# The first head group's queries in two transfers and two sums, and a new order of the opening's steps

## The chip, the cores and the metric

One core of a Trainium2 chip runs the whole program. The metric is the device time of one execution in microseconds (us), median of the runs. TensorE (PE in the views; PEld is its weight load), VectorE (DVE), ScalarE (ACT) and GpSimd (POOL) each work through their own instruction list in order. SyncE (SP) issues nearly all transfers, also in order.

## What is computed

Two things follow one another: an attention with 32 landmarks over 4 batches, 8 heads, 576 positions and 64 features, and then two feed-forward layers over 2304 tokens.

```python
q_lm, k_lm = means of q and k over 18 neighbouring positions   # 32 landmarks
A, Bm, C = softmax(q k_lm^T), softmax(q_lm k_lm^T), softmax(q_lm k^T)
Z = Bm^T / (norm1(Bm) * normInf(Bm))
for _ in range(6):
    Z = 2 * Z - Z @ Bm @ Z
x = A @ Z @ C @ v
h = x @ w_in;   x = (h * tanh(softplus(h))) @ w_out            # first layer
h = x @ w_in2;  out = maximum(h, 0)**2 @ w_out2                # second layer
```

## The kernel before

The order of all work is written out by hand: `PROGRAM` is one string of 2641 steps, and the loop at the end of the function calls them one by one. An engine's instruction list is therefore the order in which the steps of the string issue to it. No scheduler moves anything afterwards. A step reads `thing.step@room+n`: `@` names the PSUM buffer (h and y have two each, at has one), and `+n` puts n filler products of the identity matrix with itself ahead of the step on TensorE; each of them shows as two records of L312.

The things are these. The letters a to h are head groups, two per batch, with four heads each. A group's steps are: `lq`, `lk`, `lv` (loads, L492 to L528), `sq`, `sk` (landmark sums on VectorE, L547 to L563), `hq`, `hk` (the same sums begun on GpSimd, L530), `Sq`, `Sk` (a copy of a sum on ScalarE), `tq`, `tk`, `tl` (transposes on TensorE, L590, L613, L614), `Tq`, `Tk`, `TL` (their results copied out by ScalarE), `pa`, `pb`, `pc` (scores for A, Bm and C on TensorE), `cm`, `ce`, `cr` (maximum, exp and reciprocal sum for C), `pe`, `ET`, `pv`, `cv` (C times v), and `at`, `am`, `mi`, `ae`, `su`, `mu`, `tb`, `ah`, `al` (softmax of A and its split into a high and a low part). `B0`, `B1`, `B2` are the inverses: batch 0, batch 1, and batches 2 and 3 together. Their steps are `bx`, `be`, `bs` (softmax of Bm), `nr` and `rs` (norms), `n0` to `n5` with `r` and `z` (the six iterations: a product on TensorE, a copy on ScalarE, a sum on VectorE), `pw` and `wz`. `F00` and its like fold Z, C and v into the first weight matrix (`fo` on TensorE, `mh` on ScalarE, `ml` on VectorE). `p0`, `p1` and so on are chunks of the first layer's first product (`f` on TensorE, tile hc; `M` on ScalarE), `t0`, `t1` and so on its second product (`y` on TensorE, `e` adding the result to acc on ScalarE or VectorE). `U0` to `U63` are weight units of 512 KB that arrive as packed words and are turned into floats by `lo` (ScalarE), `st` (VectorE), `ab`, `cl` and `ad`. The second layer's steps begin with W, X, Q, K, Y and Z.

The opening, up to the first chunk p0, is a mesh of short steps on all engines. The first group a needs its queries and keys, the transposes, the sums, the transposed sums, then the three score products. Group a's queries are one transfer of 128x1152 floats into one half of a ring buffer, and one reduction on VectorE sums them.

Of the kernel before, what the change touches and what calls it, by code (L numbers as in the profile page):

```python
# [19 lines left out]
P = 128  # L20
# [34 lines left out]
    c.xq b.cm d.lk a.cv B0.n0@at B0.r0 B0.z0 B0.n1@y+3 U3.d@m e.lq c.zq U3.lo b.lv b.mi b.ae U1.cl U1.ad B0.r1 b.ce
    U3.st U3.ab B0.z1 B0.n2@at b.su U3.cl U3.ad b.pe@h+2 b.cr b.mu B0.r2 B0.z2 c.TL c.pc@h+1 U4.hi U4.lw d.sk b.ET
    B0.n3@y c.pb@at c.PB b.tb B0.r3 B0.z3 b.pv@y b.cv e.sq d.Sk c.pa@at B0.n4@y b.ah c.at B0.r4 B0.z4 U7.ad U7.hi c.am
    a.al d.tk@h d.tl@y+3 U5.d U5.lo c.cm B0.n5@y d.Tk d.TL d.pb@y d.PB B1.bx B0.z5 d.pc@at d.cm b.al c.ce f.lk B1.be
    B1.bs e.lk f.tk@h f.Tk d.ce d.cr c.pe@h c.ET U6.d@gh B0.pw@y B0.wz U5.st e.tk@h e.Tk B1.nr@y U5.ab B1.rs U5.cl
    U0.ad F00.fo@h F00.mh d.pe@at d.ET B1.n0@y+2 B1.z0 d.pa@at B1.r0 F00.ml U6.lo U6.st U8.d U8.lo B1.n1@y B1.z1 U8.st  # L60
    U5.ad U5.hi p0.f0 p0.f1 B1.r1 p0.f2 p0.f3 d.at U6.ab U6.cl U6.ad U8.ab p0.M0 B1.n2@y U7.lw d.am B1.z2 B1.r2 d.lv
    U6.hi p0.M1 f.lq d.pv@y f.sq B1.n3@y f.tq@at B1.r3 B1.z3 f.Tq U6.lw p0.c0 e.sk p0.g0 e.tq@h B1.n4@y e.Tq p1.f0
    B1.r4 p1.f1 p1.f2 p1.f3 d.cv U5.lw B1.z4 B1.n5@at e.Sq c.lv p0.c1 p0.g1 e.Sk e.tl@y c.pv@y p1.M0 p1.c0 c.cr B1.z5
    U11.d p1.M1 e.TL p1.g0 U8.cl U8.ad p1.c1 p1.g1 e.pb@at e.PB c.cv e.pc@h e.cm U11.lo B1.pw@y c.mi B1.wz e.ce c.ae
    f.sk c.su t0.y0 t0.e0 t0.y1 f.Sk f.Sq f.tl@at d.mi d.ae d.su f.TL e.pe@h t0.e1 f.pb@y e.ET f.pa@at f.at c.mu
    f.pc@h c.tb U9.d F10.fo@h U11.st U9.lo U9.st f.PB F10.mh c.ah d.mu c.al e.lv d.tb d.ah f.cm F10.ml U11.ab d.al
    U11.cl U9.ab U9.cl e.pa@at t0.y2 f.ce e.at e.am f.cr t0.y3 p2.f0 p2.f1 p2.M0 p2.c0 p2.f2 p2.g0 U9.ad p2.f3 p2.M1
    p2.c1 p3.f0 p2.g1 t0.e2 p3.f1 p3.M0 g.lk g.sk g.lq U10.d g.tk@at t1.y0 g.Tk U11.ad t0.e3 U10.lo U10.st U10.ab
    U13.d g.tq@at U10.cl p3.c0 f.pe@h t1.y1 p3.f2 p3.f3 U13.lo g.Sk t1.e0 f.ET g.Tq U13.st U13.ab p3.g0 U10.ad
    F01.fo@h U13.cl F11.fo@at t1.e1 F01.mh t1.y2 F11.mh U12.d U12.lo F01.ml U13.ad U13.hi U12.st U12.ab t1.y3 p4.f0  # L70
    p3.M1 p3.c1 F11.ml g.sq p4.f1 p4.f2 g.Sq p4.M0 U13.lw e.cr p3.g1 t1.e2 t1.e3 p4.f3 g.tl@y U12.cl p4.c0 p4.g0 g.TL
    p4.M1 p4.c1 p5.f0 p5.f1 g.pa@at g.pb@y U12.ad f.am U12.hi g.at g.am g.PB p5.M0 U12.lw U14.d U14.lo U14.st U14.ab
    e.pv@y+1 g.mi e.cv g.pc@at g.cm U14.cl f.lv t2.y0 p4.g1 g.ce h.lk h.sk p5.f2 p5.f3 p5.M1 U14.ad t2.y1 t2.e0 f.mi
    U15.d U14.hi h.lq t2.e1 U15.lo U15.st U15.ab U15.cl h.sq t2.y2 t2.e2 h.tk@at h.Tk h.Sk g.lv t2.y3 t2.e3 U14.lw
    g.ae g.su h.tq@at p6.f0 U15.ad U15.hi p5.c0 p5.c1 p5.g0 p6.f1 p6.f2 p5.g1 p6.f3 h.Sq h.Tq h.tl@y h.TL f.pv@y f.cv
    U31.d@T h.pb@y h.PB U15.lw B2.bx B2.be h.pc@at h.cm p6.M1 t3.y0 t3.e0 B2.bs e.mi t3.y1 t3.y2 t3.e1 h.ce U21.d
    U21.lo U17.d U21.st U21.ab h.pa@h U17.lo U17.st t3.e2 B2.nr@y t3.y3 B2.rs f.ae e.ae e.su p6.M0 B2.n0@at e.mu p6.c0
    h.at B2.r0 B2.z0 p7.f0 p7.f1 p6.c1 p6.g0 p6.g1 p7.M0 B2.n1@y B2.r1 B2.z1 p7.f2 h.lv p7.f3 p7.c0 h.am h.mi B2.n2@y
    B2.r2 B2.z2 p7.M1 h.pe@h h.ET h.cr p7.c1 g.pe@at g.ET t3.e3 f.su B2.n3@y B2.z3 B2.r3 U21.cl U21.ad t4.y0 t4.e0
    t4.y1 B2.n4@at t4.e1 B2.z4 B2.r4 h.pv@y g.pv@y B2.n5@at g.cr U17.ab g.cv h.cv e.tb p7.g1 p7.g0 h.ae B2.z5 t4.y2  # L80
    x.m f.mu U31.lo B2.pw@at B2.wz t4.y3 f.tb f.ah U30.d@T f.al t4.e2 h.su e.ah e.al t4.e3 F20.fo@at F20.mh F20.ml
    h.mu F30.fo@h F30.mh F30.ml t5.y0 t5.y1 x.e p8.f0 p8.f1 p8.f2 p8.f3 F21.fo@at t5.e1 p8.M0 p8.c0 p8.g0 t5.e0 g.mu
    t5.y2 g.tb g.ah U21.hi U31.st h.tb g.al p8.M1 h.ah h.al U31.ab p8.c1 p8.g1 t5.e2 U21.lw p9.f0 p9.f1 p9.M0 p9.f2
# [1396 lines left out]
```

## Time and profile before

| | us |
|---|---|
| median of 3 runs | 773.5 (773.37 to 775.24) |
| the profiled execution: device time | 775.11 |
| its span, first to last instruction | 773.3 |
| TensorE busy | 758.2 (98%) |
| VectorE busy | 599.3 (78%) |
| ScalarE, GpSimd busy | 377.3, 384.7 |

The profiled execution is 1.6 us above the median, and 1.8 us of it lie outside the span. A record of a TensorE instruction reaches to its modelled end, and its successor starts before that. The distance from start to start is what one costs in a dense stretch. The granted TensorE clock is 0.999 over the whole span. In a row of the timeline the first number is the start and the second the duration, both in us, and square brackets give the engine's idle time just before and what ended it.

### The profile page before, as it was taken

The numbers are of one execution on the slowest core, as the hardware profiler recorded it, in microseconds if no ns is written. First come the engines' busy times: TensorE is split into PE (matmuls) and PEld (weight loads), VectorE is DVE, ScalarE is ACT, GpSimd is POOL, SyncE is SP. The second block draws the span as 40 slices with busy tenths as digits, with TensorE's granted clock in tenths as the row PEclk, the third lists the DMA queues.
The fourth block names the chain that finished last, engine by engine and source line by source line (L and its number), as shares of the span: only waits on it lengthen the run. The fifth ranks groups of instructions, "written<-read, shape, count | busy, mean of one in ns | idle before, by whom it ended". The sixth has DMA issues, their size and how long they took to land.

```text
span 773.3 us, 15445 instructions
## 1 busy us (share of the span) xinstructions
PE 758.2 (98%) x5926; PEld 709.2 (92%) x5926; DVE 599.3 (78%) x966; ACT 377.3 (49%) x624; POOL 384.7 (50%) x269
## 2 busy tenths in 40 slices
...
GB/s 324 205 196 161 83 178 141 3 42 114 87 87 82 150 151 224 212 232 223 213 139 282 260 283 272 272 309 257 256 312 333 240 246 271 215 241 253 279 197 83
DMA packets 87721, 156.73 MB, mean 203 GB/s; under 512 B 9184, under 2 KB 37088, under 8 KB 87648
## 3 DMA queue, kind: packets, MB, share of 16 engines
...
## 4 chain that ended last, share of the span: by engine, by line
PE 89%; DVE 4%; ACT 3%; DMA 2%; issue 1%; SPq 0%; DVEq 0%; ACTq 0%
PE y L951 8%; PE y L953 8%; PE y L952 8%; PE P L1304 7%; PE P L1305 7%; PE P L1306 7%; PE O L953 4%; PE O L952 4%; PE O L951 4%; PE hc L951 4%; PE hc L952 4%; PE hc L953 4%; PE O L1379 3%; PE O L1378 3%; PE O L1377 3%; PE m L933 2%
## 5 line engine op out<-in xcount | busy, mean ns | idle before, releaser
L1198 POOL TENSOR_TENSOR ringglx<-A,ringghx 128x768 fp32r<-128x768 f32 x40 | 78.7, 1985 | 61.9 <-ACT ringghx L1193 57.1
L1002 DVE TENSOR_TENSOR ringglx<-sc,ringghx 128x576 fp32r<-128x576 f32 (+2 forms) x80 | 58.1, 747 | 18.8 <-ACT ringghx L997 18.1
L953 PE MATMUL O<-b,ringglx 128*128 128x256 f32 x240 | 67.8, 282 | 0.0
L952 PE MATMUL O<-b,ringghx 128*128 128x256 f32 x240 | 67.8, 282 | 0.0
L951 PE MATMUL O<-b,ringghx 128*128 128x256 f32 x240 | 67.7, 282 | 0.0
L1193 ACT CAST ringghx<-A 128x768 fp32r<-128x768 f32 x40 | 32.8, 835 | 69.6 <-DVE A L1175 28.9
L1036 DVE TENSOR_TENSOR acc<-acc,y 128x384 f32<-128x384 f32 x72 | 38.9, 548 | 32.7 <-PE y L953 32.6
L984 ACT ACTIVATE sc<-hc 128x576 f32<-128x576 f32 x64 | 41.4, 650 | 43.5 <-PE hc L953 39.5
L1334 DVE TENSOR_TENSOR U<-U,P 128x384 f32<-128x384 f32 x72 | 39.6, 552 | 27.8 <-PE P L1306 26.5
L997 ACT CAST ringghx<-sc 128x576 fp32r<-128x576 f32 (+2 forms) x80 | 44.7, 578 | 13.3 <-PE y L953 12.3
L953 PEld LDWEIGHTS O<-b,ringglx 128*128 128x128 f32 x240 | 45.8, 191 | 0.0
L952 PEld LDWEIGHTS O<-b,ringghx 128*128 128x128 f32 x240 | 45.8, 191 | 0.0
L951 PEld LDWEIGHTS O<-b,ringghx 128*128 128x128 f32 x240 | 45.7, 190 | 0.0
L1334 DVE TENSOR_TENSOR A<-U,P 128x384 f32<-128x384 f32 x56 | 30.7, 550 | 19.2 <-PE P L1306 16.6
L1314 ACT COPY U<-P 128x384 f32<-128x384 f32 x24 | 11.5, 480 | 68.0 <-PE P L1306 57.4
L1224 DVE TENSOR_TENSOR sum<-sum,O 128x768 f32<-128x768 f32 x32 | 30.3, 950 | 17.6 <-PE O L953 17.5
L404 POOL TENSOR_TENSOR wi<-rawwi 128x512 int32<-128x512 int32 x16 | 17.9, 1125 | 48.1 <-DVE rawwi L398 31.0
L411 POOL TENSOR_TENSOR wa<-rawwi 128x512 int32<-128x512 int32 x16 | 18.4, 1147 | 38.8 <-DVE rawwi L398 19.5
L418 POOL TENSOR_TENSOR rawwo<-rawwo 128x512 int32<-128x512 int32 x14 | 16.5, 1179 | 42.5 <-DVE rawwo L398 36.2
L1170 DVE SCALAR_TENSOR_TENSOR A<-A 128x768 f32<-128x768 f32 x28 | 32.2, 1154 | 0.4
L384 DVE SCALAR_TENSOR_TENSOR rawwo<-rawwo 128x512 uint32<-128x512 uint32 x30 | 27.5, 917 | 5.2 <-ACT rawwo L381 5.2
L1175 DVE TENSOR_TENSOR A<-A,A 128x768 f32<-128x768 f32 x28 | 29.7, 1062 | 1.2 <-DVE A L1175 0.5
...
## 6 DMA issues: line engine op xcount, KB each, us to landing
...
```

The costliest lines, as they stand in the source:

```text
L951: nc.tensor.matmul(ps, wh, rh, start=start, stop=False)
L952: nc.tensor.matmul(ps, wh, rl, start=False, stop=False)
L953: nc.tensor.matmul(ps, wl, rh, start=False, stop=stop)
L984: nc.scalar.activation(s, self.hs[hf][:, :, :CH], AF.Mish)
L997: nc.scalar.copy(self.at_ring("gh", hf, c0, e - a), self.s[hf][:, :, a:e])
L1002: nc.vector.tensor_tensor(lo, self.s[hf][:, :, a:e], hi.bitcast(F32), ALU.subtract)
L1036: nc.vector.tensor_tensor(a, a, ps, ALU.add)
L1198: nc.gpsimd.tensor_tensor(lo, self.A[self.src(k)], hi.bitcast(F32), ALU.subtract)
L1304: nc.tensor.matmul(ps[:, :TT], wh[:, c], xh[:, c, :], start=c == 0, stop=False)
L1305: nc.tensor.matmul(ps[:, :TT], wh[:, c], xl[:, c, :], start=False, stop=False)
L1306: nc.tensor.matmul(ps[:, :TT], wl[:, c], xh[:, c, :], start=False, stop=c == 1)
L1334: nc.vector.tensor_tensor(to, x, self.ps[i][:, :TT], ALU.add)
```

## The change

The transfer of group a's queries is cut in two (512 and 640 columns), each with a semaphore of its own. The sum of these queries is two reductions: the first 512 columns into 64 columns behind the data, then the other 640 with these 64. `self.first` keeps the whole buffer for that.

```diff
+                if n == "00" and nm == "q":
+                    self.first = r
                 r = r[:, : SEG * D]
-                nc.sync.dma_start(r, x)
+                for cs in (slice(0, 4 * P), slice(4 * P, 9 * P)) if n == "00" and nm == "q" else (slice(0, 9 * P),):
+                    nc.sync.dma_start(r[:, cs], x[:, cs])
...
+            elif self.n == "00" and nm == "q":
+
+                x = self.first
+                nc.vector.tensor_reduce(
+                    x[:, 9 * P : 9 * P + D], x[:, : 4 * P].rearrange("p (i d) -> p d i", d=D), AX.X, ALU.add
+                )
+                whole = x[:, 4 * P : 9 * P + D]
```

The first 1049 steps of `PROGRAM`, from the first load to the middle of chunk p23, stand in a new order. The steps themselves are the same. The fillers are fewer and elsewhere: 26 before, 23 now. The first of the lines:

```diff
-    a.lq a.sq a.tq@h+1 a.Tq a.lk a.sk a.tk@h b.lq a.Sk d.lq d.sq b.lk a.Sq a.tl@y+3 b.hq b.sq a.Tk a.TL b.tq@h b.Tq
+    a.lq a.tq@h a.lk a.Tq a.sq a.tk@h+1 b.lq b.hq a.Sq a.sk a.Sk a.tl@y b.tq@h a.Tk a.TL a.pc@h d.lq d.sq a.cm b.Tq
...
```

TensorE in the first 15 us of the program, from group a's last transposes, before (tq, tk, tl: transposes; pa, pb, pc: scores; rows on ident alone are fillers):

```order
L312 MATMUL tl_149<-ident 128x128 x3
L613 MATMUL tl_149<-ident,ringglx_77 128x128
L614 MATMUL tl_149<-ident,lmk_127 128x128
L613 MATMUL tl_149<-ident,ringghx_76 128x128
L614 MATMUL tl_149<-ident,lmq_110 128x128
L590 MATMUL tq_165<-ident,ringghx_76 128x128 x8
L312 MATMUL pa_176<-ident 128x128 x2
L737 MATMUL pa_176<-qT_122,kT_161 32x288 x8
L663 MATMUL pb_192<-kT_161,qT_122 32x32 x4
L590 MATMUL tk_199<-ident,ringglx_77 128x128 x8
L312 MATMUL pc_210<-ident 128x128 x2
L678 MATMUL pc_210<-kT_161,qT_122 32x288 x8
```

and now, from the first transposes:

```order
L600 MATMUL tq_111<-ident,ringghx_76 128x128 x8
L312 MATMUL tk_128<-ident 128x128
L600 MATMUL tk_128<-ident,ringglx_77 128x128 x8
L623 MATMUL tl_145<-ident,ringglx_77 128x128
L624 MATMUL tl_145<-ident,lmk_142 128x128
L623 MATMUL tl_145<-ident,ringghx_76 128x128
L624 MATMUL tl_145<-ident,lmq_125 128x128
L600 MATMUL tq_150<-ident,ringghx_76 128x128 x8
L688 MATMUL pc_163<-kT_159,qT_123 32x288 x8
L312 MATMUL pa_184<-ident 128x128
L747 MATMUL pa_184<-qT_123,kT_159 32x288 x8
L312 MATMUL tk_204<-ident 128x128 x2
```

The three fillers ahead of tl are gone, one stands ahead of tk and none ahead of the first transposes. Group a's pc has moved ahead of pa, of group b's tk and of pb, which now comes later than these rows.

VectorE at the same place, before (lmq, lmk: landmark sums; As: scores of A turned over; mx: maximum of C; rawwi: a weight unit):

```order
L562 TENSOR_REDUCE lmq_110<-ringghx_76 128x64
L562 TENSOR_REDUCE lmk_127<-ringglx_77 128x64
L556 TENSOR_REDUCE q_141<-q_140 128x64
L562 TENSOR_REDUCE lmq_144<-q_141 128x64
L562 TENSOR_REDUCE lmq_159<-ringghx_76 128x64
L747 STREAM_TRANSPOSE As_187<-pa_176 128x9x32 x2
L755 TENSOR_REDUCE mxa_190<-As_187 128x18
L384 SCALAR_TENSOR_TENSOR rawwi_2_197<-rawwi_2_197 128x512
L562 TENSOR_REDUCE lmk_226<-ringglx_77 128x64
L686 TENSOR_REDUCE mx_235<-pc_210 128x1
```

and now:

```order
L559 TENSOR_REDUCE ringghx_76<-ringghx_76 128x64
L572 TENSOR_REDUCE lmq_125<-ringghx_76 128x64
L572 TENSOR_REDUCE lmk_142<-ringglx_77 128x64
L566 TENSOR_REDUCE q_173<-q_172 128x64
L572 TENSOR_REDUCE lmq_176<-q_173 128x64
L696 TENSOR_REDUCE mx_179<-pc_163 128x1
L697 TENSOR_SCALAR mx_179<-mx_179 128x1
L757 STREAM_TRANSPOSE As_194<-pa_184 128x9x32 x2
L765 TENSOR_REDUCE mxa_197<-As_194 128x18
L384 SCALAR_TENSOR_TENSOR rawwi_2_200<-rawwi_2_200 128x512
L572 TENSOR_REDUCE lmq_215<-ringghx_76 128x64
L572 TENSOR_REDUCE lmk_225<-ringglx_77 128x64
```

One reduction is added at the head, the maximum of C has moved ahead of the scores of A, and group b's query sum behind both.

VectorE around the start of the last inverse, B2, before (acc: sums of the first layer's output; rawwo_9, rawwi_9: units U21 and U17; nr, c: norms of B2):

```order
L1036 TENSOR_TENSOR acc_1149<-acc_1149,y_1919 128x384
L384 SCALAR_TENSOR_TENSOR rawwo_9_1949<-rawwo_9_1949 128x512
L393 TENSOR_SCALAR rawwo_9_1949<-rawwo_9_1949 128x512
L384 SCALAR_TENSOR_TENSOR rawwi_9_1952<-rawwi_9_1952 128x512
L1036 TENSOR_TENSOR acc_1350<-acc_1350,y_1932 128x384
L848 TENSOR_REDUCE nr_1999<-nrm_1968 128x8
L852 SCALAR_TENSOR_TENSOR c_2001<-nr_1999 128x4
```

and now:

```order
L837 TENSOR_TENSOR inv_1923<-braw_735,sb_1924 128x128
L838 STREAM_TRANSPOSE inv_1923<-inv_1923 128x128
L1046 TENSOR_TENSOR acc_1186<-acc_1186,y_1908 128x384
L1046 TENSOR_TENSOR acc_1262<-acc_1262,y_1932 128x384
L858 TENSOR_REDUCE nr_1966<-nrm_1946 128x8
L862 SCALAR_TENSOR_TENSOR c_1968<-nr_1966 128x4
```

The three instructions on the weight units U21 and U17 no longer stand between the two acc sums.

## Rows read from the trace of the kernel before

**Rows 1.** The page: busy us, share of the span and instructions.

```profile
PE 758.2 (98%) x5926; PEld 709.2 (92%) x5926; DVE 599.3 (78%) x966; ACT 377.3 (49%) x624; POOL 384.7 (50%) x269
```

**Rows 2.** Stretches of the opening: length, busy us by engine, clock, DMA share, GB/s.

```profile
5.00:10.00 5.00, 5.00 (x25) 5.00 (x25) 5.00 (x3) 2.06 (x4) 2.01 (x2) 1.00 1.03 412
10.00:15.00 5.00, 5.00 (x68) 3.90 (x66) 4.20 (x8) 3.83 (x9) 2.51 (x3) 1.00 1.01 384
15.00:20.00 5.00, 3.25 (x30) 3.06 (x29) 4.72 (x11) 4.35 (x10) 2.85 (x3) 1.00 1.07 303
20.00:30.00 10.00, 8.53 (x164) 6.34 (x162) 9.29 (x29) 8.02 (x17) 2.55 (x3) 1.00 0.73 255
30.00:40.00 10.00, 10.00 (x217) 7.95 (x206) 9.55 (x21) 6.76 (x20) 7.80 (x7) 1.00 0.50 141
40.00:60.00 20.00, 18.88 (x323) 14.99 (x323) 18.79 (x48) 18.62 (x37) 8.32 (x8) 1.00 0.61 191
60.00:80.00 20.00, 19.86 (x264) 16.64 (x263) 19.29 (x38) 17.13 (x36) 10.23 (x9) 1.00 0.45 141
```

**Rows 3.** Waits of TensorE over the whole span: us, times, longest.

```profile
PE tq L590 <- DMA ringghx<-in_q_dram: 2.5, 1, 2.5
PE pe L703 <- ACT E L692: 1.8, 1, 1.8
...
PE y L951 <- DVE acc L1036: 1.0, 1, 1.0
PE tl L636 <- DVE inv L859: 0.8, 1, 0.8
```

**Rows 4.** Timeline: the first loads used, on TensorE and GpSimd.

```profile
4.73 1.97 PE L590 MATMUL tq<-ident,ringghx 128*128 128x128 f32 x8 [2.47 <-DMA ringghx<-in_q_dram]
...
7.78 1.00 POOL L537 TENSOR_TENSOR ringghx<-ringghx 128x384 f32<-128x384 f32 x1 [5.84 <-DMA ringghx<-in_q_dram]
```

**Rows 5.** Timeline: VectorE's first reductions, and its first wait after them.

```profile
4.71 2.13 DVE L562 TENSOR_REDUCE lmq<-ringghx 128x64 f32<-128x1152 f32 x1 [2.69 <-DMA ringghx<-in_q_dram]
...
8.83 1.50 DVE L556 TENSOR_REDUCE q<-q 128x64 f32<-128x768 f32 x1
...
10.37 0.95 DVE L562 TENSOR_REDUCE lmq<-q 128x64 f32<-128x448 f32 x1
...
12.78 0.85 DVE L747 STREAM_TRANSPOSE As<-pa 128x288 f32<-128x288 f32 x2 [0.73 <-PE pa L737]
```

**Rows 6.** Timeline: eight transposes at the slow and the fast pace, and fillers.

```profile
8.20 1.49 PE L312 MATMUL tl<-ident 128*128 128x128 f32 x6
...
12.66 1.10 PE L590 MATMUL tk<-ident,ringglx 128*128 128x128 f32 x8
```

**Rows 7.** Timeline: group a's C, from scores to transposed exponentials.

```profile
14.13 0.88 PE L678 MATMUL pc<-kT,qT 64*32 64x288 f32 x16
...
17.63 0.86 PE L703 MATMUL pe<-ident,E 128*96 128x128 f32 x6 [1.75 <-ACT E L692]
```

**Rows 8.** Timeline: first and last iteration of B0, first low part.

```profile
29.77 0.43 PE L869 MATMUL nw__456<-inv 32*32 32x64 f32 x16
...
41.44 0.42 PE L869 MATMUL nw__669<-inv 32*32 32x64 f32 x16 [0.35 <-DVE inv L886]
...
49.70 1.22 DVE L947 TENSOR_TENSOR ml<-m,mh 128x1024 fp32r<-128x1024 f32 x1
```

**Rows 9.** The chain that ended last, near 130 us: start, us, what.

```profile
121.20 8.10 DMA rawwi<-in_moe_w_in_dram
129.38 0.68 ACT rawwi L381
130.09 0.69 DVE rawwi L384
130.78 0.48 DVE acc L1036
131.30 0.44 PE y L951
```

More of the change, by code (lines that the diff above doesn't have):

```diff
@@ L55 @@
[L55 to L83, printed above, removed]
-    p9.f3 p9.M1 t5.y3 p9.c0 p9.g0 p10.f0 U30.lo U30.st p10.f1 p10.f2 p9.c1 p9.g1 p10.M0 t5.e3 t6.y0 F21.mh F21.ml
@@ L85 @@
-    U19.d U19.lo p10.f3 p11.f0 U19.st U19.ab U19.cl p10.M1 U19.ad t6.e0 t6.y1 t6.e1 U17.cl U17.ad F31.fo@at U25.d@T
-    U25.lo U24.d@T U24.lo x.m U25.st t6.y2 t6.y3 U24.st t6.e2 t6.e3 p10.c0 p10.g0 p10.c1 p10.g1 U24.ab p11.f1 p11.f2
-    U31.cl p11.M0 p11.c0 p11.f3 U25.ab p11.M1 p11.c1 t7.y0 t7.y1 U26.d U25.cl U25.ad U26.lo U26.st t7.e0 t7.e1 t7.y2
-    t7.y3 t7.e2 U24.cl U16.d p11.g1 U16.lo F31.mh p11.g0 U31.ad U16.st U26.ab U26.cl U26.ad t7.e3 U16.ab U16.cl U16.ad
-    p12.f0 p12.f1 t8.y0 t8.e0 F31.ml p12.M0 p12.c0 p12.g0 U34.d@T U34.lo p12.f2 p12.f3 p12.M1 t8.y1 p12.c1 p13.f0
@@ new lines @@
+    t1.y3 g.sq U12.ab U12.cl p4.M0 g.Sq U13.hi g.tl@y g.TL F11.ml p3.M1 p3.c1 p4.f2 p4.f3 p5.f0 p5.f1 p3.g1 U13.lw
+    g.pa@at t1.e3 U12.ad U12.hi U12.lw g.at p4.M1 p4.c0 p4.c1 g.pb@y U14.d g.PB p4.g0 e.pv@y e.cv g.pc@at t2.y0 U14.lo
+    p4.g1 g.cm t2.y1 g.ce U14.st U14.ab h.lk p5.M0 g.am p5.f2 p5.f3 U14.cl t2.e0 t2.e1 p5.M1 p6.f0 p6.f1 h.tk@at h.sk
+    U15.d t2.y2 f.cr U15.lo U15.st h.Sk U15.ab U14.ad U14.hi e.mi e.ae g.mi U15.cl g.ae h.Tk t2.y3 t2.e2 h.lq t2.e3
+    h.tq@at h.sq h.Sq U15.ad U15.hi h.tl@y p6.f2 p6.f3 U31.d@T g.lv h.Tq p5.c0 p5.g0 h.TL f.pv@y p5.c1 U15.lw U24.d@T
@@ new lines @@
+    h.pb@y h.PB B2.bx p5.g1 U14.lw f.cv h.pc@at h.cm U21.d f.am t3.y0 t3.y1 t3.e0 B2.be B2.bs p6.M0 t3.y2 t3.e1
+    B2.nr@y t3.e2 U21.lo B2.rs f.mi p6.M1 h.pa@h f.ae t3.y3 t3.e3 h.at p7.f0 p7.f1 h.ce e.su B2.n0@at p6.c0 p6.c1
+    p6.g0 p7.f2 p7.f3 U24.lo B2.r0 B2.z0 p7.M0 B2.n1@y g.pe@at g.su U25.d@T B2.r1 B2.z1 B2.n2@y e.mu h.cr U30.d@T
+    B2.r2 B2.z2 h.pe@h+1 B2.n3@y B2.z3 p6.g1 t4.y0 U21.st U21.ab B2.r3 t4.y1 h.ET g.ET t4.e0 B2.n4@at g.cr h.am h.mi
+    t4.e1 B2.z4 p7.M1 h.pv@y p7.c0 p7.g0 g.pv@y B2.r4 B2.n5@at g.cv g.mu g.tb B2.z5 g.ah f.su f.mu h.cv e.tb t4.y2
@@ new lines @@
+    p7.c1 t4.e2 B2.pw@at U25.lo t4.y3 B2.wz F20.fo@at F20.mh f.tb F30.fo@h t4.e3 p7.g1 f.ah t5.y0 t5.e0 t5.y1 t5.y2
+    f.al F30.mh h.ae F30.ml e.ah e.al U25.st t5.e1 F20.ml p8.f0 p8.f1 p8.f2 p8.M0 p8.f3 p9.f0 h.su h.mu h.tb t5.e2
+    p8.M1 g.al h.ah h.al p9.f1 p9.f2 t5.y3 F21.fo@at p8.c0 p8.c1 p8.g0 p8.g1 U17.d t5.e3 U17.lo U17.st U17.ab p9.M0
+    p9.c0 p9.f3 p10.f0 U21.cl p9.M1 p9.c1 p9.g0 p9.g1 p10.f1 p10.f2 p10.M0 U21.ad U21.hi t6.y0 t6.e0 t6.y1 t6.y2
+    U17.cl U30.lo U21.lw U30.st U30.ab t6.e1 U30.cl U19.d F21.mh F21.ml U25.ab p10.f3 p10.M1 p11.f0 p11.f1 t6.y3
```

76 lines of the change are left out of this document (48 added, 28 removed).

## The prediction

> **What bounds the kernel now.** I read the page first. TensorE is busy 98% of the span and no other engine more than 78% [rows 1], so after the opening the time is TensorE's work plus its waits. The change reorders the first part of the program and removes no real work, so all it can give is waits. The list of TensorE's waits [rows 3] has the long ones, and four are where steps moved: 2.5 us for the first queries, 1.8 for the exponentials of group a's C, 1.0 for an acc sum near 131 us, 0.8 for the norms of B0. That would make 6 us, but the table by stretch [rows 2] says who sets the pace there. From 5 to 80 us VectorE is busy 5.00, 4.20, 4.72, 9.29, 9.55, 18.79 and 19.29 us, that is 70.84 of 75; it idles 4.16 us, pauses between instructions included. TensorE looks full in some of these stretches too, but its records overlap and include fillers. So up to 80 us VectorE's queue is the bound, and a TensorE wait that goes is worth only what it brings forward on VectorE. Past 80 us TensorE is the bound and a wait of its own counts in full.
>
> **The change, part by part.** The base is the profiled execution, 775.1 us, 1.6 above the median of 773.5; I take differences from it and put them on the median.
>
> *The split transfer.* VectorE and TensorE wait for the first queries until 4.71 and 4.73 [rows 4, 5]. Group b's queries are the third transfer of 576 KB in the queue and are first used at 7.78 by GpSimd, which had been idle [rows 4]. So two transfers take 3.05 us and one 1.52. At that pace the second piece, 320 of 576 KB, takes 0.85 us, and the first is there at 4.73 - 0.85 = 3.88. That holds if the queue already flows; the other end is that the start-up of a transfer hides all of it and the first piece comes at 4.73. I take 3.9, as the pace is that of the same queue. The sum now is two reductions. 448 columns took 0.95 us and 768 took 1.50 [rows 5], so 1.72 ns a column: 512 columns 1.06, 704 columns 1.39, together 2.45 against 2.13 for the one of 1152. The queries' sum ends at 3.9 + 2.45 = 6.35 instead of 4.71 + 2.13 = 6.84: 0.5 us earlier, or 0.3 later at the other end. The next reductions wait for transfers that queue one issue later, so I take 0.4 earlier.
>
> *Group a's C ahead of its A.* TensorE's wait of 1.75 us ahead of pe at 17.63 [rows 7] comes from pc standing behind pa, pb and group b's tk. Now pc follows group b's tq, and its exponentials are ready some 2 us earlier. This is a gain on TensorE and hardly one on VectorE. Its steps ahead of the first low part ml, which starts at 49.70 [rows 8], are the same ones in both orders, plus the added reduction: only a score product of TensorE and copies of ScalarE lie on different sides of it. So ml comes earlier by the 0.4 us above and by what VectorE idles less. Its longest idle piece after the start, 0.73 us at 12.78 [rows 5], is a wait for group a's scores. It now waits for pc in place of pa, with group b's query sum (384 columns, about 0.8 us at the pace above) no longer ahead of the wait: this piece is 0.6 to 1.3 us now. Later, group b's TL must come through ScalarE before bx, where VectorE before had a weight unit's st to do. I put idle gained and lost at nil. The bounds: 0.6 us lost; or half of the 4.16 idle gained, 2.1, as the rest is pauses and the start.
>
> *The iterations of B0.* They run from 29.77 to 41.44 [rows 8], 2.3 us each for products of 0.43. What lies between is other work on VectorE's queue, and nearly all of it stands there still, so nothing.
>
> *Fillers.* Three fewer, two records each, 0.11 us a record at the fast pace: 0.66 us at most. Nearly all stand where VectorE is the bound, so nothing.
>
> *Units U21 and U17 near 130 us.* Here TensorE is the bound. The chain [rows 9] shows a transfer of U17 issued at 121.20 that takes 8.10 us, ScalarE's lo at 129.38, VectorE's st at 130.09, and only then acc, which frees the PSUM buffer that TensorE wants: TensorE waits 1.0 us [rows 3] until 131.30. In the new order no weight unit stands on VectorE between the two acc sums. U17 comes about a hundred steps later, and U24 and U21, whose transfers replace it, are worked on by VectorE only after the third iteration of B2. The wait of 1.0 should be gone. The bounds: nothing gained, if ScalarE, which still has U21's lo in its queue ahead of a chunk's M, passes the late transfer on to TensorE instead; and 1.2 gained, with the pause at the new start.
>
> *After 160 us* the order changes too, but TensorE hardly waits there; nothing, within 0.5 either way.
>
> The sum: -0.4 + 0 + 0 + 0 - 1.0 = -1.4 us. On the profiled execution 773.7, on the median **772.1**.
>
> **The rivals.**
>
> *More of it arrives.* VectorE's idle shrinks by its bound of 2.1, since pc earlier lets E, ET and cv come without waits: -0.4 - 2.1 - 1.0 - 0.3 for fillers = -3.8, giving 769.7. For it: four waits of TensorE and one of VectorE stand just where steps moved. Against it: VectorE is 94% busy from 5 to 80 us and got more work. It counts as faster from 771.2 down.
>
> *Slower: TensorE stays at its slow pace.* Eight transposes take 1.97 us at 4.73 [rows 4] and 1.10 at 12.66 [rows 6]; these are the 1.2 and the 2.4 GHz level, although the granted clock reads 1.00 in both stretches [rows 2]. Between them TensorE worked without a hole from 4.73, with six filler records at 8.20 [rows 6]. Now these six are gone: TensorE has a hole until the keys land and another, by my estimate about 0.8 us (its reduction less the fillers that stood there), until group a's sum of keys is copied, ahead of tl. If the pace does not rise before about 22 us, the real work from 10.8 to 22 takes double. TensorE is busy there 4.2 + 3.25 + 1.7 = 9.15 us [rows 2]; less 20 filler records (2.2) and 0.9 of overlap it is 6.0. So 6.0 us more, of which the old wait of 1.75 takes up its part: +4.25, and -1.0 for the wait at 131 stays: 773.5 + 3.2 = 776.7. It decides if the fast pace comes later than about 20 us; up to 14 us it costs about 1 and the time stays within 0.3%.
>
> The Trainium skill (TensorE: Matmul & The Clock Gate, part 4 on PE-mode transpose) holds that transposes do not count as busy for the clock in the way that products do. This trace does not decide it, as fillers stood between the transposes and the faster pace; by that rule this rival is what happens at least until pc and pa, the first products of the new order, have run.
>
> *Nothing arrives.* The first piece lands no earlier, the second reduction costs 0.3, ScalarE carries U21's wait to TensorE, and the idle shift gives back 0.2: 773.4.
>
> **How the numbers follow.** Forecast as summed: 0.50, with an own range of 771.0 to 773.2. More arrives: 0.20. Nothing arrives: 0.17. Slow pace: 0.13. A measurement of this kernel can tell about 0.3% (2.3 us) from no change, so faster means below 771.2 and slower above 775.8. Faster: 0.20 of the second case and 0.05 of the forecast's edge, 0.25. Slower: 0.13. Within: 0.62. The range leaves out about half of the case with more, below 769.8, and the larger part of the slow case, above 775.8.
>
> **What would show it.** In the profile after: the first transposes at 3.9, in two runs of four, and the queries' sum ending near 6.4. VectorE's busy share from 5 to 80 us still 94% or more, and ml 0.4 us earlier. The wait of TensorE for acc near 131 us gone, and none of about 1 us in its place between 120 and 140. The pace of eight transposes at 1.1 us from about 11 us on. I am wrong if ml starts before 48 or after 51, if a set of eight transposes after 15 us still takes nearly 2, or if new waits show past 140 us, where I count none.

## The result, and the profile after

The changed kernel is slower: 778.41 us against 773.91 for the kernel before on the same chip, ratio 1.0056 with a 95% interval of 1.0046 to 1.0066. The same kernel run again (e12 below) gave 1.0063 (1.0049 to 1.0078). One execution of the kernel before took 1899.54 us; the ratio leaves it out. So by the ratios the change costs 4.3 to 4.9 us where I had forecast a gain of 1.4, and the time lies outside the range.

The page of the changed kernel, its first lines on busy time, answers [rows 1]:

```profile
PE 760.2 (98%) x5920; PEld 709.9 (91%) x5920; DVE 591.6 (76%) x967; ACT 374.9 (48%) x622; POOL 383.3 (49%) x269
```

TensorE is busy as long as before; the span is 777.2 instead of 773.3. The table by stretch, to be laid beside [rows 2] (length, then busy us of TensorE, its weight load, VectorE, ScalarE, GpSimd; clock, DMA share, GB/s):

```profile
5.00:10.00 5.00, 2.91 (x14) 2.45 (x12) 2.88 (x2) 1.16 (x2) 0.42 (x1) 1.00 0.99 354
10.00:15.00 5.00, 4.73 (x48) 3.05 (x47) 3.52 (x6) 3.41 (x6) 3.60 (x4) 1.00 1.01 386
15.00:20.00 5.00, 3.61 (x37) 3.20 (x38) 4.85 (x9) 3.56 (x8) 1.76 (x2) 1.00 1.08 302
20.00:30.00 10.00, 7.95 (x123) 6.49 (x122) 7.21 (x21) 6.51 (x16) 2.60 (x2) 0.83 0.78 259
30.00:40.00 10.00, 10.00 (x157) 8.23 (x159) 9.35 (x29) 8.21 (x19) 5.07 (x5) 1.00 0.56 161
40.00:60.00 20.00, 18.79 (x345) 13.78 (x330) 18.89 (x48) 17.39 (x38) 10.42 (x10) 1.00 0.65 192
60.00:80.00 20.00, 19.92 (x333) 16.14 (x327) 18.75 (x36) 17.10 (x37) 10.21 (x9) 1.00 0.37 114
```

VectorE's column adds up to 65.45 of the 75 us, against 70.84 before. It had been the engine that sets the pace here, and 5.4 us of new idle time stand in it, most of them ahead of 30 us. Where they come from stands in VectorE's timeline (start, duration, and in brackets the idle time before and what ended it), as against [rows 5]:

```profile
3.49 1.03 DVE L559 TENSOR_REDUCE ringghx<-ringghx 128x64 f32<-128x512 f32 x1 [1.47 <-DMA ringghx<-in_q_dram]
4.55 1.36 DVE L572 TENSOR_REDUCE lmq<-ringghx 128x64 f32<-128x704 f32 x1
8.04 2.14 DVE L572 TENSOR_REDUCE lmk<-ringglx 128x64 f32<-128x1152 f32 x1 [2.12 <-DMA ringglx<-in_k_dram]
...
13.93 0.76 DVE L696 TENSOR_REDUCE mx<-pc 128x1 f32<-128x576 f32 x1 [1.02 <-PE pc L688]
...
23.27 0.22 DVE L818 TENSOR_REDUCE mxb<-braw 128x2 f32<-128x64 f32 x1 [1.20 <-ACT braw L677]
...
27.59 0.85 DVE L757 STREAM_TRANSPOSE As<-pa 128x288 f32<-128x288 f32 x2 [1.18 <-PE pa L747]
...
53.68 1.22 DVE L957 TENSOR_TENSOR ml<-m,mh 128x1024 fp32r<-128x1024 f32 x1
```

The first queries are summed at 5.9 instead of 6.84, but then VectorE waits 2.12 us for the keys, which land at 8.0. Before, they were there when it came to them:

```profile
6.76 2.16 DVE L562 TENSOR_REDUCE lmk<-ringglx 128x64 f32<-128x1152 f32 x1
```

Three more waits of over 1 us follow, and the first low part ml starts at 53.68 instead of 49.70 [rows 8]. That is 4.0 us, and the two profiled executions differ by 3.8 in all, so the loss stands before 54 us.

The wait for acc near 131 us [rows 3, 9] is gone from TensorE's list of waits, as forecast. A new one of 0.50 us stands at 168.47, for ScalarE's Mish of a chunk (its activation function, `M`). So two of the signs of being wrong that the prediction named came: ml after 51 us, and a new wait past 140.

### The profile page after: what moved, and what is told of

Same layout as the page of the kernel before. It is cut to its first block, busy times and chain, and to the rows that moved or that the text cites. A ratio compares the mean times of both kernels' runs of the same rounds, so it can differ in the third digit from the quotient of the medians.

```text
span 777.2 us, 15434 instructions
## 1 busy us (share of the span) xinstructions
PE 760.2 (98%) x5920; PEld 709.9 (91%) x5920; DVE 591.6 (76%) x967; ACT 374.9 (48%) x622; POOL 383.3 (49%) x269
## 4 chain that ended last, share of the span: by engine, by line
PE 91%; ACT 2%; DVE 2%; issue 2%; DMA 2%; POOL 0%; SPq 0%; DVEq 0%; ACTq 0%; POOLq 0%
PE y L961 9%; PE y L962 8%; PE y L963 8%; PE P L1314 7%; PE P L1316 7%; PE P L1315 7%; PE O L963 4%; PE O L962 4%; PE O L961 4%; PE hc L961 4%; PE hc L963 4%; PE hc L962 4%; PE O L1389 3%; PE O L1388 3%; PE O L1387 3%
## 5 line engine op out<-in xcount | busy, mean ns | idle before, releaser
L1012 DVE TENSOR_TENSOR ringglx<-sc,ringghx 128x576 fp32r<-128x576 f32 (+2 forms) x80 | 55.8, 719 | 15.8 <-ACT ringghx L1007 15.5
L384 DVE SCALAR_TENSOR_TENSOR rawwi<-rawwi 128x512 uint32<-128x512 uint32 x32 | 26.9, 843 | 4.9 <-ACT rawwi L381 4.9
```

Source lines behind the costliest of these rows:

```text
L1012: nc.vector.tensor_tensor(lo, self.s[hf][:, :, a:e], hi.bitcast(F32), ALU.subtract)
```

## The experiments

Each ratio is to the kernel before on the same chip, with its 95% interval; 0.1% is 0.77 us.

**The split alone, and the new order alone.** The first kernel has the loads and sums of the changed kernel and the `PROGRAM` of before, the second the reverse:

```diff
 # e1_old_split: from the changed kernel
-PROGRAM = (new order)
+PROGRAM = (order of before)
 # e2_new_single: from the kernel before
-PROGRAM = (order of before)
+PROGRAM = (new order)
```

Expected of the first: 

> The order of before, with only the split transfer and the two sums. In the changed kernel's trace the first keys landed 1.9 us later than before (8.0 instead of 6.1 us) although they are issued only 0.47 us later. Theory A, the split itself slows the queue behind it: the keys land at 7.5 to 8.1 us here too, VectorE's sum of keys starts then instead of at 6.8, and the time is 1.0 to 2.0 us above before (about 775). Theory B, the late keys belong to that one execution or to the new order: the keys land at 6.1 to 6.6 us and the time is within 0.5 us of before.

Expected of the second: 

> The new order, with the one transfer and the one sum of before. Theory A (the split delays the keys): the keys land at 6.1 to 6.6 us, TensorE's full pace comes at about 11 instead of 12.8 us, and the time falls by 1.5 to 2.5 us from the changed kernel's 778.4, to about 776.5. Theory B (late keys by chance or by the new order): the keys still land near 8 or vary, and the time stays within 0.7 us of 778.4.

Measured: the split alone 1.0028 (1.0017 to 1.0039), the new order alone 1.0023 (1.0015 to 1.0032). Together that is 0.51% of the 0.56 and 0.63% of the changed kernel: two losses that nearly add up in the time, and neither part gains. VectorE of the split alone (first fence), of the new order alone (second), and of the order of before at the two waits that the new order has (third):

```profile
3.60 1.04 DVE L559 TENSOR_REDUCE ringghx<-ringghx 128x64 f32<-128x512 f32 x1 [1.59 <-DMA ringghx<-in_q_dram]
...
8.36 2.13 DVE L572 TENSOR_REDUCE lmk<-ringglx 128x64 f32<-128x1152 f32 x1 [2.34 <-DMA ringglx<-in_k_dram]
...
51.54 1.22 DVE L957 TENSOR_TENSOR ml<-m,mh 128x1024 fp32r<-128x1024 f32 x1
```

```profile
4.64 2.13 DVE L562 TENSOR_REDUCE lmq<-ringghx 128x64 f32<-128x1152 f32 x1 [2.63 <-DMA ringghx<-in_q_dram]
6.69 2.15 DVE L562 TENSOR_REDUCE lmk<-ringglx 128x64 f32<-128x1152 f32 x1
...
21.31 0.22 DVE L808 TENSOR_REDUCE mxb<-braw 128x2 f32<-128x64 f32 x1 [1.20 <-ACT braw L667]
...
40.15 1.54 DVE L556 TENSOR_REDUCE q<-q 128x64 f32<-128x768 f32 x1 [1.19 <-DMA q<-in_q_dram]
...
51.49 1.22 DVE L947 TENSOR_TENSOR ml<-m,mh 128x1024 fp32r<-128x1024 f32 x1
```

```profile
21.47 0.21 DVE L808 TENSOR_REDUCE mxb<-braw 128x2 f32<-128x64 f32 x1
...
38.00 1.52 DVE L556 TENSOR_REDUCE q<-q 128x64 f32<-128x768 f32 x1
```

Theory A's mechanism held in both: with the cut the keys come at 8.4, a little later than I expected, without it VectorE goes from the queries straight to the keys at 6.69. The split also costs a little more than the 1.0 to 2.0 us that I gave it (0.28% is 2.2). The split moves the first ml by 1.84 us, the new order by 1.79, the latter through two waits of 1.2 us that the order of before did not have.

Two cautions. One profile shows one execution: with the opening of before, the first ml came at 49.70 (before), 49.76 (e4 below) and 48.84 (e6 below), so a difference of less than 0.9 us at that place says little. And at ml the two losses don't add: 1.84 and 1.79 make 3.6, while the changed kernel's ml is 4.0 late in the profile above and 2.4 late in a second one (52.13, e12 below). The second of the new order's waits, for group e's queries, isn't in the changed kernel at all: its VectorE comes to them later, at 42.10, and they are there.

**What of a cut costs.** Two kernels in the order of before cut a transfer in another way:

```diff
 # e5_old_rows: the first queries by partitions
-                nc.sync.dma_start(r, x)
+                for ps in (slice(0, 64), slice(64, 128)) if n == "00" and nm == "q" else (slice(0, 128),):
+                    nc.sync.dma_start(r[ps, :], x[ps, :])
 # e11_old_keys_cut: the first keys by columns, the queries whole
-                nc.sync.dma_start(r, x)
+                for cs in (slice(0, 4 * P), slice(4 * P, 9 * P)) if n == "00" and nm == "k" else (slice(0, 9 * P),):
+                    nc.sync.dma_start(r[:, cs], x[:, cs])
```

> The order and the one sum of before; the first queries again come in two transfers, but cut by partitions (0 to 63, 64 to 127), so that every packet keeps the 4608 bytes of before, where the cut by columns makes packets of 2048 and 2560. In three kernels with the cut by columns the keys landed at 8.0 to 8.3 us. Theory D1, the smaller packets unsettle the queue: here the keys land at 6.0 to 6.6 us and the time is within 0.5 us of before. Theory D2, a further transfer at the head of the queue is enough: the keys land after 7.3 us and the time is 1 to 2.5 us above before.

> Before, with group a's keys (the second transfer) cut in two by columns, 512 and 640, and the first queries in one transfer again; the sums are those of before. Theory J, any cut near the head delays what stands behind it: the first queries land at 4.7 as before, but the second piece of the keys after 7 us and group b's queries (7.63 before) after 9 us, and the time is 1 to 2.5 us above before. Rival, only a cut of the very first transfer does it, since the queue is still starting up there: the keys land at 6.1 to 6.5, group b's queries by 8.1, and the time is within 0.5 us of before.

Measured: 1.0023 (1.0014 to 1.0033) and 1.0013 (1.0004 to 1.0022). The stretch from 3 to 8 us of five kernels, one row each, in the order before, new order with one transfer, changed kernel, cut by partitions, keys cut (columns as above, the last two DMA share and GB/s):

```profile
3.00:8.00 5.00, 3.27 (x16) 3.27 (x17) 3.29 (x2) 1.01 (x1) 0.23 (x1) 1.00 1.01 401
```

```profile
3.00:8.00 5.00, 3.24 (x16) 3.27 (x17) 3.36 (x2) 1.16 (x2) 0.38 (x1) 1.00 1.02 414
```

```profile
3.00:8.00 5.00, 2.37 (x10) 2.07 (x10) 2.39 (x2) 1.16 (x2) 0.00 (x0) 1.00 0.94 331
```

```profile
3.00:8.00 5.00, 1.91 (x9) 1.78 (x10) 1.94 (x1) 0.00 (x0) 0.00 (x0) 1.00 0.99 311
```

```profile
3.00:8.00 5.00, 3.27 (x16) 3.28 (x17) 3.29 (x2) 1.01 (x1) 0.00 (x0) 1.00 1.00 374
```

The engines of the queue are busy in all five, but with a cut they move 311 to 374 GB/s instead of 401 to 414. At 331 against 401 the changed kernel is short of 0.35 MB by 8 us. With the cut by columns it is the transfers behind the cut that lack them. With the cut by partitions it is the cut transfer itself: the first queries are whole only at 6.06 instead of 4.71, and the keys, which land at 7.7, are taken without a wait (e5):

```profile
6.06 2.13 DVE L563 TENSOR_REDUCE lmq<-ringghx 128x64 f32<-128x1152 f32 x1 [4.04 <-DMA ringghx<-in_q_dram]
8.11 2.15 DVE L563 TENSOR_REDUCE lmk<-ringglx 128x64 f32<-128x1152 f32 x1
```

By partitions the packets keep their 4608 bytes, so small packets are not needed for the loss (theory D1 fell, D2 held); whether the two cuts slow the queue for the same reason is not shown. When the keys were cut their second piece was not late (VectorE took them at 6.75 without a wait), which theory J had said it would be; group b's queries behind them were (GpSimd starts on them at 8.88 instead of 7.78 [rows 4]). What is left of J is its first half: what stands behind a cut by columns arrives 1 to 2 us later. Why the queue slows is not shown; the traces only show that some packets of the transfer after the cut take several times as long as the rest. Nor do these two profiles account for the times: the first ml comes at 50.34 and 49.82, that is 0.6 and 0.1 us late, where the times are 1.8 and 1.0 us longer.

**By which engine the split costs.** With the split in the order of before, TensorE has nothing from 5.6 to 8.4 us; fillers were put there:

```diff
 # e14_old_split_fill: from the split alone
-a.sk a.tk@h b.lq
+a.sk a.tk@h+5 b.lq
```

> The order of before with the split (776.54 us), and 5 fillers ahead of a's tk, where TensorE has nothing from 5.6 to 8.4 us while it awaits the keys; there the full pace came at 12.4 instead of 10.8. Theory K, the split costs through TensorE's late pace: the pace comes before 11 us and the time falls by 1.5 us or more, below 775.1. Theory L, it costs through VectorE, whose sums start 1.6 us later and which is busy without a pause behind them: the pace comes earlier too, but VectorE's wait of 0.60 us for pa is all that can go, and the time falls by 0.6 us at most, to 775.9 or above.

Measured: 1.0034 (1.0022 to 1.0046), not below the 1.0028 without fillers. The clock rose at 7.1 us and VectorE's wait of 0.60 for pa went, so ml came 0.6 us earlier in that execution (50.93), but the keys still came at 8.42 and the time did not fall. So theory K fell and L is left: the split costs through VectorE's late sums, not through TensorE's pace.

**The granted clock.** In the profile of the changed kernel the clock falls back. The two stretches behind TensorE's hole at 20.5, of the changed kernel and of the same kernel run again (the number ahead of the DMA share is the clock):

```profile
20.00:23.00 3.00, 1.33 (x16) 0.86 (x15) 2.00 (x5) 2.58 (x8) 2.52 (x2) 1.00 1.02 291
23.00:27.00 4.00, 4.00 (x68) 3.63 (x76) 2.83 (x10) 2.70 (x7) 0.08 (x1) 0.57 0.82 316
```

```profile
20.00:23.00 3.00, 1.32 (x16) 0.85 (x15) 1.72 (x5) 2.58 (x9) 2.26 (x2) 1.00 1.02 292
23.00:27.00 4.00, 3.33 (x94) 2.44 (x93) 3.68 (x13) 2.70 (x6) 0.00 (x0) 1.00 0.93 343
```

Same instructions, same hole; once the clock falls to the 1.2 GHz level from 23.0 to 26.4 us, once it stays at 2.4. The first ml starts at 53.68 in the one and at 52.13 in the other, and the spans are 777.2 and 775.1 us. Four kernels went after this: fillers in the late hole, fillers in the early ones, the kernel again, and early fillers with one step of the order mended:

```diff
 # e3_new_fill_late: from the changed kernel
-b.tl@y b.TL ... b.pb@at b.PB
+b.tl@y+4 b.TL ... b.pb@at+3 b.PB
 # e10_new_fill_early: from the changed kernel
-a.lq a.tq@h ... a.tk@h+1 ... a.tl@y
+a.lq a.tq@h+1 ... a.tk@h+5 ... a.tl@y+3
 # e12_after_again: no edit
 # e13_new_mended: as e10, and
-a.pb@y a.PB d.tq@h b.Sq b.tl@y
+b.Sk b.Sq ... a.pb@y a.PB d.tq@h b.tl@y
```

> The changed kernel with fillers added in two holes of TensorE: 4 ahead of group b's tl (they run from about 20.2) and 3 ahead of its pb (from about 21.9). Nothing else is changed. Theory C, the hole from 20.5 to 22.6 us, filled only in part by short work, is why the granted clock is 0.50 from 23.0 to 26.4 us in the changed kernel: here it stays at 1.00, tk, pv and pa behind it take 1.07, 0.88 and 0.5 us instead of 1.91, 1.26 and 0.72, and the time falls by 1.3 to 2.0 us to about 776.7. Rival: VectorE sets the pace there and the lost clock costs nothing, or the drop has another cause: the time stays within 0.5 us of 778.4.

> The changed kernel (778.4 us) with fillers added in TensorE's holes of the first 11 us: 1 ahead of the first transposes, 5 instead of 1 ahead of group a's tk (the hole from 6.0 to 8.06 while the keys are awaited), 3 ahead of its tl. Theory I, the full pace came at 12.8 to 13.7 us, 2 to 3 us later than before, because TensorE had these holes: here it comes before 11.5 us, VectorE's wait of 1.02 us for pc at 13.9 falls below 0.4, and the time falls by 0.6 to 1.2 us. Rival: the pace follows the real work, which starts with the keys at 8.06, or the late keys hold VectorE whatever TensorE's pace: no earlier rise, or one that moves the time by less than 0.4 us.

> The changed kernel once more, unchanged, for a second profile. Theory C1, the granted clock of 0.50 from 23.0 to 26.4 us belongs to this kernel, after its hole of TensorE from 20.5 to 22.6: it shows again, n0 of B0 comes at 33.5 us or later. Theory C2, it fell into that one execution: the clock stays at 1.00 after its rise, n0 comes at 32.4 to 33.0, as in the kernels with fillers (32.8), while the keys land at 8.0 to 8.5 again; the median is 777 to 778.5 either way.

> The changed kernel, split kept, with the early fillers (1, 5 and 3 ahead of a's tq, tk and tl) and with b.Sq behind b.Sk. If the parts add: 778.4 less 1.9 for the early fillers less 1.1 for b.Sq, 775.4, with the full pace before 11.5 us, VectorE's wait for braw below 0.8 us and the first ml at 52.0 to 52.4. Rival, the two mends pay for the same wait: 776 or more.

Measured: 1.0042 (1.0026 to 1.0058), 1.0036 (1.0024 to 1.0049), 1.0063 (1.0049 to 1.0078), 1.0040 (1.0027 to 1.0053). The profile again showed no fall, so C2 holds for the profile. But the mean clock that goes with every run tells more: it was 0.998 or less in 7 of the 12 runs of the changed kernel (mean time 778.8 us; 777.2 for the other 5), and in none of the 16 runs of these three kernels with fillers. In the profiles the sign is good: the two with a mean clock of 0.998 (the changed kernel's and e8's below) have a fall ahead of the last 3 us, and the fifteen others, at 0.999 or 1.000, have none. So the fall is a matter of chance that this kernel meets in about half of its executions, at a price of some 1.7 us, and that it met in none with fillers in its holes. Theory C had about the right price for one fall and took for certain what is frequent; in the time of the kernel with late fillers alone it can't be told (0.14% less than the changed kernel, with intervals that overlap). That it is this hole that invites the fall is not shown: the kernel with early fillers alone keeps it (TensorE busy 1.30 of the 3 us from 20) and met no fall in 5 runs.

That early fillers bring the fast pace earlier (theory I) isn't shown: with the same fillers it came at 6.75 us in one kernel and at 12.9 in the other. TensorE's transposes of group a's keys, early fillers alone and with b.Sq moved:

```profile
5.36 1.95 PE L312 MATMUL tk<-ident 128*128 128x128 f32 x10
8.56 1.10 PE L600 MATMUL tk<-ident,ringglx 128*128 128x128 f32 x8 [1.25 <-DMA ringglx<-in_k_dram]
```

```profile
5.20 2.34 PE L312 MATMUL tk<-ident 128*128 128x128 f32 x10
8.58 1.97 PE L600 MATMUL tk<-ident,ringglx 128*128 128x128 f32 x8 [1.04 <-DMA ringglx<-in_k_dram]
```

What I had expected of the last kernel fell: by its parts, early fillers and b.Sq moved, it should have come to some 775.4 us, and at 776.96 it is no faster than with the fillers alone (0.40 against 0.36%). Its 0.40% is as much as 0.28% for the split and 0.13% for the order with b.Sq moved (below).

**The new order's own loss.** All four kernels have one transfer and one sum.

```diff
 # e7_new_b_sq: from e2
-b.Sk ... a.ET a.pb@y a.PB d.tq@h b.Sq b.tl@y
+b.Sk b.Sq ... a.ET a.pb@y a.PB d.tq@h b.tl@y
 # e8_new_b_sq_e_sq: from e7
-e.lq e.sq c.pa@at c.at U7.hi d.tl@y B0.r4 B0.z4
+e.lq c.pa@at c.at U7.hi d.tl@y B0.r4 B0.z4 e.sq
 # e9_new_e_lq: from e7, the load alone
-U3.d@m U3.lo ... d.lk ... b.lv ... U5.d ... e.lq e.sq
+U3.d@m e.lq U3.lo ... d.lk ... b.lv ... U5.d ... e.sq
 # e15_new_c_pa: from e7
-b.tb d.tk@h+3 B0.n4@y b.ah c.PB ... e.lq e.sq c.pa@at c.at
+b.tb c.PB c.pa@at d.tk@h+3 B0.n4@y b.ah ... e.lq c.at e.sq
```

> The new order with one transfer and one sum (775.9 us), and one step moved: b.Sq, the copy of group b's query sum on ScalarE, stands right behind b.Sk instead of behind a's ET and the copy of a's pb. Theory G, VectorE's wait of 1.20 us for braw at 21.3 us comes from this copy, which was held up behind ET (ScalarE 18.59 to 19.27): TensorE's wait of 0.96 for lmq is gone, VectorE's wait falls below 0.4, the first ml comes 0.7 to 1.2 us earlier than the 51.49 of that kernel, and the time falls to 774.8 to 775.3. Rival, another wait of VectorE takes its place: ml within 0.3 us of 51.49, time within 0.4 us of 775.9.

> As the kernel with b.Sq moved, and e.sq (group e's query sums, two reductions of VectorE) five steps later, behind B0's z4, since VectorE waited 1.19 us there for the transfer of these queries. Theory G: that wait is gone too, ml comes at 49.3 to 50.3 us, near the 49.70 of before, and the time is 773.6 to 774.4, that of before. Rival: ml within 0.4 us of the kernel with b.Sq alone, since the iterations of B0 wait elsewhere.

> The new order with one transfer, one sum and b.Sq moved (774.84 us), and one more step moved: e.lq, the load of group e's queries, stands ahead of U3.lo, where before had it, instead of behind U5.d, d.lk and b.lv in SyncE's queue. Theory H: in that kernel VectorE waits 1.58 us at 39.67 for these queries, whose transfer is issued at 34.72; loaded earlier they are there, the wait is gone, the fifth iteration's sum and n5 (43.08) come 1.2 to 1.6 us earlier, ml comes at 49.4 to 49.9, and the time is 773.2 to 773.9. Rival: the buffer is not free any earlier, or the earlier transfer holds up those behind it (b's values, d's keys): the time stays within 0.4 us of 774.84.

> The kernel with one transfer, one sum and b.Sq moved (0.13% above before, first ml at 50.98), with group c's c.PB and c.pa ahead of d.tk and n4 on TensorE, as before had them, and c.at ahead of e.sq on VectorE. Theory M, two things are late together there, group e's queries (VectorE waits 1.58 us for them at 39.67) and c's scores, which stand behind d.tk and n4: to move the one alone only exposed the other (the kernels with e.sq or e.lq moved); with c's scores early VectorE turns them over within that wait, the sum behind n4 comes at 42.0 to 42.2 instead of 42.85, ml at 50.1 to 50.4, and the time falls by 0.5 to 0.9 us, to within 0.1% of before. Rival, c's scores ahead hold up d.tk and n4 by as much as VectorE gains: ml within 0.3 us of 50.98.

Measured: 1.0013 (1.0004 to 1.0021), 1.0066 (1.0053 to 1.0079), 1.0032 (1.0020 to 1.0045), 1.0023 (1.0014 to 1.0032).

The first wait can be read from the trace. In the new order the copy of group b's query sum stands on ScalarE behind other work and last behind the copy of a's exponentials: the sum is there at 15.98, the copy runs at 19.35, and ScalarE is busy in between. ScalarE of the new order with one transfer (e2):

```profile
18.59 0.77 ACT L711 COPY ET<-pe 96x768 f32<-96x768 f32 x1
19.27 0.17 ACT L667 COPY braw<-pb 128x32 f32<-128x32 f32 x1
19.35 0.24 ACT L576 COPY lmq<-lmq 128x64 f32<-128x64 f32 x1
...
20.54 0.68 ACT L381 ACTIVATE ringglx<-ringglx 128x512 f32<-128x512 uint32 x1
21.11 0.17 ACT L667 COPY braw<-pb 128x32 f32<-128x32 f32 x1
```

Moving that one copy forward (e7) took 0.10% off the ratio, as theory G had it, but the intervals overlap. VectorE's wait only fell from 1.20 to 0.71, not below 0.4: the lo of U7 (at 20.54 above) still stands ahead of the copy of b's scores. The starts of B0's first and last product on TensorE and of the first ml tell more:

| kernel | first product of B0 | last product of B0 | first ml |
|---|---|---|---|
| before | 29.77 | 41.44 | 49.70 |
| new order, one transfer (e2) | 30.55 | 43.58 | 51.49 |
| and b.Sq moved (e7) | 29.67 | 43.08 | 50.98 |
| and e.sq later (e8) | 29.55 | 41.59 | 53.29 |
| e7 and e.lq earlier (e9) | 30.32 | 43.48 | 51.38 |
| e7 and c.pa earlier (e15) | 29.93 | 42.85 | 50.73 |

With b.Sq moved the first product is back where it was before, so the first wait is mended there.

The second wait, 1.2 to 1.6 us for group e's queries, did not yield in the time. With their sum later, VectorE waits for c's scores instead (first row, e8); with the load earlier, too (second, e9), and group b's values then land late for TensorE (third, also e9); with c's scores earlier (fourth, e15) 1.12 us of waiting stay:

```profile
40.58 0.85 DVE L747 STREAM_TRANSPOSE As<-pa 128x288 f32<-128x288 f32 x2 [2.61 <-PE pa L737]
```

```profile
42.47 0.85 DVE L747 STREAM_TRANSPOSE As<-pa 128x288 f32<-128x288 f32 x2 [1.31 <-PE pa L737]
```

```profile
38.76 0.86 PE L718 MATMUL pv<-v,ET 96*32 96x64 f32 x44 [0.83 <-DMA v<-in_v_dram]
```

```profile
39.47 0.85 DVE L747 STREAM_TRANSPOSE As<-pa 128x288 f32<-128x288 f32 x2 [1.12 <-PE pa L737]
```

The kernel with the sum later is a case of its own. Its last product of B0 comes at 41.59, level with before, so the wait for group e's queries was what held B0. But the sum now stands ahead of VectorE's next maximum of scores, TensorE waits for the exponentials made with it, and in this execution its clock is at the 1.2 GHz level from 46.7 to 50.2 us (the number ahead of the DMA share):

```profile
46.34 1.17 PE L703 MATMUL pe<-ident,E 128*96 128x128 f32 x6 [2.45 <-ACT E L692]
```

```profile
47.00:50.00 3.00, 3.00 (x20) 2.53 (x19) 2.15 (x11) 1.89 (x4) 0.00 (x0) 0.50 0.46 139
```

The mean clock is 0.998 or less in 4 of its 5 runs (mean 779.1 us, 777.0 for the other), so its 0.66% is in part the price of such falls.

So at 38 to 46 us several things are late together in the new order, and the wait that the profile names is only the last of them. Theories G (its second half), H and M fell in the time; what would bring the new order level with that of before there is open.

**The part past 73 us.** One kernel moves U17 alone, the other takes the new order from t0's first y on:

```diff
 # e4_old_units: from the kernel before
-U21.ab h.pa@h U17.lo U17.st t3.e2 B2.nr@y t3.y3 B2.rs
+U21.ab h.pa@h t3.e2 B2.nr@y t3.y3 B2.rs U17.lo U17.st
 # e6_old_then_new: the first 282 steps of before, then the rest in the new order
```

> Before, with one move: U17.lo and U17.st stand behind B2's rs instead of ahead of the acc sum of t3. If the prediction's step on the acc wait was right: TensorE's wait of 1.0 us near 131 is gone, and the time is 0.7 to 1.2 us below before (772.3 to 772.8). Rival: another wait takes its place within the next 10 us (ScalarE with U17's lo late, n0 of B2 behind st), and the time stays within 0.4 us of before.

> One transfer, one sum. The first 282 steps in the order of before (up to the first y of t0, about 73 us), then all others in the new order. Theory F, the whole loss of the new order lies in its first 282 steps: at 72 us it stands as before, the acc wait of 1.0 near 131 us is gone, the new wait of 0.66 for ScalarE near 168 us comes, and the time is within 0.6 us of before. Rival, the order after 73 us loses too: the time is 1 us or more above before.

Measured: 0.9998 (0.9990 to 1.0006) and 0.9997 (0.9988 to 1.0006). TensorE's first y behind the norms of B2, in the kernel that moves U17 (this kernel's lines are numbered differently: L682 is L840 of before, L793 is L951):

```profile
129.97 0.45 PE L682 MATMUL nrm<-inv 32*32 32x32 f32 x32
130.35 0.45 PE L793 MATMUL y<-ringghx,wo_4h 128*128 128x384 f32 x1
```

The wait of 1.0 us is gone; y follows the norms at once, and the first product of B2 comes at 132.65 instead of 133.60. Yet the median moves by -0.16 us, and the interval reaches from -0.8 to +0.5. So the mechanism is shown and its 0.95 us in the time is not. In that execution 0.6 us went again at 682 us, in a wait for a transfer of the second layer's weights. And the wait itself differs from execution to execution: with the same steps at that place it is 1.00 us before, 0.81 in e14, 0.22 in e11, 0.19 in e5 (the row below), and none in e1, with transfers of U17 that took 8.10, 7.90, 7.31, 7.28 and 7.14 us.

```profile
131.14 0.44 PE L952 MATMUL y<-ringghx,wo_4h 128*128 128x384 f32 x1 [0.19 <-DVE acc L1037]
```

The second kernel shows that the new order past 73 us neither gains nor loses anything that can be measured: it drops the wait at 131 and takes one for ScalarE, whose Mish runs behind a table load:

```profile
162.95 0.40 PE L951 MATMUL hc<-three3x,mh 128*128 128x288 f32 x1 [0.50 <-ACT sc L984]
```

Theory F held: the whole loss of the new order lies in its first 282 steps. This kernel, 773.43 us against 773.77, is the fastest of all that ran, by less than can be told.

## Why the prediction was wrong

- *What bounds the kernel.* Right: VectorE sets the pace from 5 to 80 us. What the changed kernel loses there shows as VectorE's idle time, and fillers that sped up TensorE alone brought nothing in the order of before (e14).
- *The split transfer.* This is the first step that failed. The first piece came at 3.5, earlier than my 3.9, and the sum ended at 5.9 instead of 6.35. I priced what stands behind it with "transfers that queue one issue later", that is 0.1 us of my 0.5, and gave the whole term +0.3 as its worse end. The runs show +1.84 at the first ml and 0.28% of the time (in the 4 of 11 runs whose mean clock shows no fall, 0.22%). I had worked out the pace of the first piece from two whole transfers and taken the same pace for the rest; but the pace itself falls when a transfer is cut, from 401 to 331 GB/s over 3 to 8 us. That VectorE, having summed early, would just wait for the keys could be seen even without that: in the trace of before they land at 6.12 and are used at 6.76, so an earlier sum could gain no more than 0.64 us.
- *Group a's C ahead of its A.* The second step that failed. I saw that TL of group b must come through ScalarE ahead of bx, and still put "idle gained and lost at nil", with 0.6 as the worse end. It lost 1.8 us at ml and 0.23% of the time. The order as such put a's C earlier, if by 1.4 us and not by 2 (pe at 16.27 instead of 17.63 with one transfer), and the wait for pc came out at 0.73, within my 0.6 to 1.3. But I compared which steps stand ahead of ml on VectorE and not when ScalarE and SyncE deliver what they read. Two inputs came late: a copy that now stood further back in ScalarE's list, and a load that SyncE issues behind three other steps, d.lk, b.lv and U5.d (at 34.7 us instead of 23.3).
- *The iterations of B0.* "Nothing" was wrong by the same waits: with one transfer the first one came 0.8 us later and the last one 2.1 (43.58 instead of 41.44).
- *Units U21 and U17.* The mechanism was right, at its place: TensorE no longer waits there, and moving U17 alone brings the first product of B2 0.95 us forward. In the time of the kernel that does this alone it can't be found. I had read the 1.0 us from one execution; in five with these steps it was between 0 and 1.0, so the term of -1.0 was too large for the median.
- *After 160 us.* A new wait of 0.5 us, for ScalarE behind a table load. What it costs can't be told: the kernel that has the new order past 73 us alone (e6) is level with before.
- *The slow pace.* This rival gave 776.7, nearest to the result, and its mechanism is a part of it only, so its number is near by luck. The pace rose at 11.9 and 12.8 us in the two profiles, after 10.75 before, which by my own point of decision costs about 1. What it did not have is a clock that falls again at 23, some 1.7 us in about half of the executions. In the new order with one transfer and b.Sq moved (e7) TensorE ran nothing but transposes and two filler records from 4.74 us on, and it was at the fast pace by 8.25, as its timeline shows by the first tl (0.27 instead of 0.42 us) and the next eight tq (1.04 instead of 1.94):

```profile
6.48 0.63 PE L312 MATMUL tk<-ident 128*128 128x128 f32 x2
6.90 1.50 PE L590 MATMUL tk<-ident,ringglx 128*128 128x128 f32 x8
8.25 0.27 PE L613 MATMUL tl<-ident,ringglx 128*128 128x128 f32 x1
...
9.53 1.04 PE L590 MATMUL tq<-ident,ringghx 128*128 128x128 f32 x8
```

  The rule of the Trainium skill that stood beside this rival (TensorE: Matmul & The Clock Gate, part 4 on PE-mode transpose), that transposes do not count as busy in the way that products do, does not agree with these rows; by it only the two filler records could have raised the pace before pc at 10.61.
- *The range.* It was made from bounds for each term that all looked at the rows of the moved step itself. Both large errors lay with what was behind it in another engine's queue, and they had the same sign.
